# Two of GT's token tiles change places, and q's raw weights are loaded behind the first loads of Wv and Wo

## The chip, the cores and the metric

The kernel is one program on one core of a Trainium2 chip. The metric is the device time of one execution in microseconds, as the median of the runs. Names of engines are those of the profile: PE is TensorE's matmuls, PEld its weight loads, DVE is VectorE, ACT ScalarE, POOL GpSimd and SP SyncE, which in this kernel only issues DMAs.

## The reference

All tensors are float32; S = 2048 tokens, D = 640 channels, F = 1536, and 32 heads of 20 channels.

```
g = sigmoid((x * gate_w).sum(-1, keepdims=True))
q, k, v = heads of x @ wqkv
pq, pk = phi(q), phi(k)          # phi(t) = where(t > 0, t + 1, exp(t)) + 1e-6
kv = einsum("bhsd,bhse->bhde", pk, v);  z = sum of pk over the tokens
a = (pq @ kv / (pq . z + 1e-6), heads joined) @ wo
b = (sigmoid(x @ w_gate) * (x @ w_up)) @ w_down
out = g * a + (1 - g) * b
```

## The kernel before

The products run on PE in three passes each: an operand is split into a high part (a copy on ACT, line 420) and a low part (the difference, on DVE, line 424), and high*high, high*low and low*high are summed in PSUM (`mm3`, lines 407 to 409). Most of the large products are cut into blocks in Strassen's manner (seven block products), which needs sums of blocks on DVE ahead of the splits.

Instead of forming v, the kernel forms GT = x^T phi(k), of 640 x 640, from token tiles, and multiplies by Wv afterwards: kv = Wv^T GT for each group of heads. M = kv Wo then stands for the whole way from phi(q) to the output. The program goes like this:

1. phi(k) is formed for 16 token blocks of 128 rows. For each there is a token tile of 4 x 640 floats in each partition: the split x and the split phi(k). A pool `p1` holds six of these, with the tags tok0 to tok5, side by side in SBUF in this order; `token_tile()` hands them out in turn by a list of six tags.
2. GT is summed in batches. The last batch (c = 3) works on six token tiles: two of block 5, two of block 6, two of block 7. It goes over GT's seven pieces (five of 128 rows and two strips) for block 5 first, then over all seven for block 6, then over all seven for block 7. Each pass over the pieces is what lets go of a block's token tiles.
3. The pool `p1` is closed, and its memory is given to the pools of the next stage: `pw` and `pw2` (weights and intermediate tiles) and `mp` (Wv, Wo and kv). A tile there has to wait for the last reader of the token tile that lay in its place. In `mp` lie, from the bottom up, three buffers for Wv's groups (`wv_sb`), two for Wo's (`wo_sb`), then Wo's split parts (`woh`, `wol`), then kv's parts (`kvt`, `kvh`, `kvl`). `wst` in `pw2` holds raw weights: those of q first, then those of the gated unit.
4. The next stage starts with q for token groups 2 and 3 (`q_unit`, tile `wg` as weights, `dd` and `rot` as PSUM), and mixed into this stand six times `kv_part` (ten small matmuls with `wv_sb`, line 1627; then DVE masks the result into `kvt` and splits it) and `m_part` (Wo's split parts times kv). `wo_split` makes `woh` and `wol` from `wo_sb` on ACT and DVE.

What PE, ACT and DVE do is written out in a fixed order, which a small planner (`Order`) decides as the program is built, by estimated times for each engine. Each engine takes its instructions in that order, and a wait holds all that stands behind it. SP's queue is a list as well: the DMAs are issued in the order in which they stand, and one that waits for a tile to come free holds the ones behind it. In the built program an engine waits for a count in a semaphore; a DMA on SP also waits for the eighth DMA before it.

Around the change, SP's queue holds these loads: `xz` (x for the next chunk), `wg` and `w` (split and raw weights of q, the last ones that belong to GT's stage), then q's raw weights `wst`, then three loads of Wv (`load_mv`), two of Wo (`load_mo`), then `ws` and `wu` (q's other split weights) and a second `wst`. The line `sp.t = max(sp.t, freed)` sets only the planner's own estimate of when SP gets there.

Of the kernel before, what the change touches and what calls it, by code (L numbers as in the profile page):

```python
# [365 lines left out]
P_LAG, A_LAG, V_LAG = 0.2, 0.18, 0.14  # L366
# [8 lines left out]
def gated_mix_kernel(ctx: ExitStack, tc: tile.TileContext, xt, xn, wk, wv, wo, wst_q, wst_f, out_t):  # L375
# [6 lines left out]
    order = Order()  # L382
    rings = Rings()
    sp, gp = Ring(nc.sync, order, rings, 0, 0.38, 1.5), Ring(nc.gpsimd, order, rings, 1, 0.55, 2.2)
# [105 lines left out]
    tok_n = []  # L490

    def token_tile(dt=F32R):

        tag = f"tok{(0, 3, 1, 4, 2, 5)[len(tok_n) % 6]}"
        tok_n.append(0)
        return p1.tile([P, 4, D], dt, name="tok", tag=tag)

# [185 lines left out]
    for n in range(6):  # L683
        p1.tile([P, 4, D], F32, name="first", tag=f"tok{n}")
    st = [token_tile(F32).rearrange("p a b -> p (a b)") for _ in range(2)]
    k3h, k3l = (p1.tile([P, 2, HW], F32R, name=n, tag="kr", bufs=5) for n in ("k3h", "k3l"))
    wk_st = [st[k // 3][:, k % 3 * 2 * HW:(k % 3 + 1) * 2 * HW] for k in range(KC)]
# [66 lines left out]
    def queue_ls():  # L754

        p, w = FC // 2 - 1, 4 * P
        wd_dram[p] = dram.tile([P, 2, WF], F32, name=f"wd{p}")
        raw = qs.tile([P, 2, D], F32, name="qraw", tag="qraw")[:, :, :w]
        for j in range(2):
            sp.dma_start(raw[:, j], wst_f[2 * p + j, :, 2, :w])  # L760
        (a11, a21), (a12, a22) = [raw[:, j].rearrange("p (q h c) -> h p q c", q=2, h=2) for j in range(2)]

        def sums(part):
            if part == 0:
                add(a22, a21, a22)
                sub(a21, a11, a21)
            else:
                sub(a11, a22, a11)
                sub(a12, a12, a11)

        high = {}

        def form(j, q):
            if q == 0:
                high[j] = qs.tile([P, 2, 2 * P], F32R, name="qp", tag="qp", bufs=2)
            src = raw[:, j, 2 * q * P:2 * (q + 1) * P]
            split(high[j][:, q], src.bitcast(F32R), src)
            if q:
                cs = slice(2 * D + j * w, 2 * D + (j + 1) * w)
                order.then(lambda: [gp.dma_start(wd_dram[p][:, i, cs], t) for i, t in  # L780
                                    enumerate((f32(high[j]).rearrange("p q c -> p (q c)"), raw[:, j]))])
        for part in range(2):
            order.add(0, 2 * v_cost(2 * P), lambda part=part: sums(part), "qw", None, kept=True)
        for j in range(2):
            for q in range(2):
                order.add(a_cost(2 * P), v_cost(2 * P), lambda j=j, q=q: form(j, q), "qw", None, kept=True)
# [54 lines left out]
    def split_xn(n):  # L841
        i = tok(n // 2, n % 2)
        if i not in TOK:
            TOK[i] = token_tile()
        XN[i] = (TOK[i][:, 0], TOK[i][:, 1])
        split(*XN[i], xn_st.pop(n)[0])
        order.then(lambda: load_xn(n + 3))
# [118 lines left out]
    def k_split(i, after=""):  # L966
        r = KR.pop(i)
        if i not in TOK:
            TOK[i] = token_tile()
        PK[i] = (TOK[i][:, 2], TOK[i][:, 3])  # L970
        vh, vl = (t.rearrange(view2, j=2) for t in PK[i])
        act(vh, r, AF.Copy, after, bias=EPS)
        at = order.act + A_LAG

        def low():
            order.vec = max(order.vec, at)
            vec3(vl, r, EPS, f32(vh), OP.add, OP.subtract)
        order.then(low)
# [151 lines left out]
    for c in range(1, 4):  # L1130
# [102 lines left out]
        if c == 3:  # L1233
            for u in range(first, NU):
                g.part(u, 0, 2, ("cc", "dd", "rot", "cc")[u - first])
                order.fill()
            freed = order.pe + P_LAG
        for u in range(NU):
            g.part(u, 2 if u in g.ps else 0, 4, ("rot", "dd", "ch", "cc", "dd", "rot", "rot")[u])
            order.fill()  # L1240
# [2 lines left out]
            if c == 2 and u == NU - 1:  # L1243
                queue_ls()
    order.need(("xn", 7))
    order.need(("pk", 7))

    for u in (KC, KC + 1, 1):
# [36 lines left out]
    def load_form(n, i):  # L1285
        t = (wg_tile, wu_tile, ws_tile)[i]()
        w = t.shape[2]
        for c0, c1 in ((0, 2 * P), (7 * P, w), (5 * P, 7 * P), (2 * P, 5 * P)) if n == ("f", 0, 0) and i == 2 else ((0, w),):
            sp.dma_start(f32(t[:, :, c0:c1]), w_dram[n[::2] + (i,)][:, :, c0:c1])
        put(n, i, t)  # L1290
# [6 lines left out]
    def load_w():  # L1297
        t = pw2.tile([P, 2, D], F32, name="wst", tag="wst", bufs=2)
        if not w_loads:
            t = t.rearrange("p k c -> p (k c)").rearrange("p (k c) -> p k c", c=CW)  # L1300
            sp.dma_start(t, xt[len(c1_x), :, :, CW:])
            c1_x.append(t)
            other[-1].at = order.when(t)
            return
        n = w_loads.pop(0)
        sp.dma_start(t, wst_f[n[2], :, 0:2] if n[0] == "f" else wst_q[:, 0:2])
        WST[n] = t
        W_AT[n] = t
# [245 lines left out]
            for g in gs2:  # L1554
                order.add(0, v_cost(TG), lambda g=g, u=u: one(g, u), "den", lambda g=g, u=u: order.when(st[g, u]) + 1.5, chain=True)

    sp.t = max(sp.t, freed)
    load_w()
    mp_cm = tc.tile_pool(name="mp", bufs=1, reuse_waits="tile")
    mp = mp_cm.__enter__()  # L1560
    MV, MO, MO_AT, ZP = {}, {}, {}, []
# [1 line left out]
    def hg_slice(hg):  # L1563
        h0, h1 = HG[hg:hg + 2]
        return h0 * DH, (h1 - h0) * DH
# [8 lines left out]
    def load_mo(hg):  # L1574
        if hg < NHG:
            c0, w = hg_slice(hg)
            o = mp.tile([bdn, D], F32, name="wo_sb", tag="wo_sb", bufs=2)
            sp.dma_start(o[:w], wo[c0:c0 + w])
            MO[hg] = o
            MO_AT[hg] = o[:w]  # L1580
# [75 lines left out]
    load_mv(2)  # L1656
    load_mo(0)
    load_mo(1)
    sp.t = max(sp.t, order.pe + P_LAG)
    load_form(("q", 1, 2), 2)  # L1660
    load_form(("q", 1, 2), 1)
# [1401 lines left out]
```

## Time and profile before

| | |
|---|---|
| median of 3 runs | 730.3 us (730.19 to 730.45) |
| the profiled execution: its own time | 731.26 us |
| the profiled execution: its span, first to last instruction | 729.5 us |
| PE busy | 720.3 us, 99% of the span, 3395 matmuls |
| DVE / ACT / POOL busy | 583.0 us (80%) / 370.7 us (51%) / 117.2 us (16%) |
| mean granted clock of TensorE | 0.998 |
| data moved by DMA | 191.95 MB, 263 GB/s in the mean |

A row of the timeline is: start, duration, engine, line, operation, output <- inputs, shape, and in brackets the idle time of the engine before it and what ended it. The three rows of one product (lines 407, 408, 409) overlap in the record, since matmuls are pipelined; the distance from start to start is what a matmul costs. "issue" on SPq is the time in which the queue handles the DMA, not the transfer. DMA share is the mean busy share of the core's 16 DMA engines.

### The profile page before, as it was taken

To read this page: it belongs to the slowest core of one execution; us is meant where nothing else is said; L and a number is where in the kernel's file an instruction comes from. 1 tells how busy PE (TensorE), PEld (TensorE's weight loads), DVE (VectorE), ACT (ScalarE), POOL (GpSimd) and SP (SyncE) were. 2 spreads that over 40 slices of the span, in tenths; PEclk is the share of its full clock that TensorE was granted. 3 is DMA by queue.
4 is the path that set the end of the run, shared out by engine and by line. 5 is a ranking of instruction groups with operands and counts; after the bars stand their busy time and mean duration, and the time that the engine had idled before them with its cause. 6 is when DMAs were issued, how large, how long until landed. Compare 5 with 4: busy or idle time off the path is not lost.

```text
span 729.5 us, 9892 instructions
## 1 busy us (share of the span) xinstructions
PE 720.3 (99%) x3395; PEld 606.1 (83%) x3395; DVE 583.0 (80%) x1009; ACT 370.7 (51%) x685; POOL 117.2 (16%) x189
## 2 busy tenths in 40 slices
PE   9999999989999999999999999999999999999998
PEld 7999898768788888888888888888888888888886
DVE  6888878767768889898989987347696968799895
ACT  6784748148646763635354854355423242444451
POOL 0211113213320221311211134001010101002200
PEclk9999999999999999999999999999999999999999
DMA  7677688696967866757787979968989895959957
GB/s 249 167 217 191 179 200 249 181 318 233 342 228 273 313 230 243 274 207 271 272 294 284 299 269 354 411 236 276 356 251 302 270 396 175 409 216 333 213 105 238
DMA packets 78889, 191.95 MB, mean 263 GB/s; under 512 B 8394, under 2 KB 37018, under 8 KB 75126
## 3 DMA queue, kind: packets, MB, share of 16 engines
q1 hardware_dynamic: 57654, 117.72, 49.2%
q0 software_dynamic: 20896, 73.36, 30.0%
q8 instruction: 27, 0.44, 0.2%
q10 hardware_dynamic: 288, 0.23, 0.1%
q14 instruction: 24, 0.20, 0.1%
HBM read 113.46 MB, written 75.52 MB: 259 GB/s over the span
## 4 chain that ended last, share of the span: by engine, by line
PE 91%; issue 3%; DMA 2%; DVE 1%; POOL 1%; ACT 1%; SPq 0%; POOLq 0%; DVEq 0%; ACTq 0%
PE ch L408 10%; PE ch L407 10%; PE ch L409 10%; PE cc L407 8%; PE cc L409 8%; PE cc L408 8%; PE dd L407 6%; PE dd L408 6%; PE dd L409 6%; PE rot L407 5%; PE rot L409 5%; PE rot L408 5%; DMA wo_sb<-wo 1%; DMA p_dram<-qe 1%; PE dd L2788 1%
## 5 line engine op out<-in xcount | busy, mean ns | idle before, releaser
L420 ACT ACTIVATE c<-ch 128x512 f32<-128x512 f32 x54 | 32.2, 596 | 82.0 <-PE ch L409 81.7
L424 DVE TENSOR_TENSOR hf<-c,hf 128x512 fp32r<-128x512 f32 x80 | 54.4, 686 | 19.3 <-ACT hf L420 18.9
L420 ACT ACTIVATE hf<-c 128x512 fp32r<-128x512 f32 x80 | 48.9, 624 | 31.1 <-DVE c L424 31.0
L424 DVE TENSOR_TENSOR c<-cc,c 128x512 f32<-128x512 f32 x42 | 28.9, 688 | 26.4 <-PE cc L409 16.8
L407 PE MATMUL ch<-xth,ws 128*128 128x512 f32 x112 | 43.8, 391 | 0.1
L408 PE MATMUL ch<-xtl,ws 128*128 128x512 f32 x112 | 43.6, 390 | 0.0
L409 PE MATMUL ch<-xth,ws 128*128 128x512 f32 x112 | 43.6, 389 | 0.0
L424 DVE TENSOR_TENSOR c<-c,c 128x512 f32<-128x512 f32 x52 | 35.7, 686 | 3.3 <-ACT c L420 2.7
L424 DVE TENSOR_TENSOR tb<-rot,tb 128x512 f32<-128x512 f32 x56 | 36.1, 680 | 0.4 <-PE rot L409 0.4
L407 PE MATMUL dd<-xrh,wg 128*128 128x512 f32 x90 | 35.2, 391 | 0.0
L408 PE MATMUL dd<-xrl,wg 128*128 128x512 f32 x90 | 35.1, 389 | 0.0
L409 PE MATMUL dd<-xrh,wg 128*128 128x512 f32 x90 | 35.0, 389 | 0.0
L420 ACT ACTIVATE c<-dd 128x512 f32<-128x512 f32 x22 | 13.1, 598 | 41.1 <-PE dd L409 41.1
L407 PE MATMUL cc<-xbh,ws 128*128 128x512 f32 x84 | 32.8, 390 | 0.0
L408 PE MATMUL cc<-xbl,ws 128*128 128x512 f32 x84 | 32.7, 389 | 0.0
L409 PE MATMUL cc<-xbh,ws 128*128 128x512 f32 x84 | 32.7, 389 | 0.0
L424 DVE TENSOR_TENSOR tb<-dd,tb 128x512 f32<-128x512 f32 x36 | 24.7, 686 | 9.3 <-PE dd L409 9.3
L420 ACT ACTIVATE dd<-ch 128x512 f32<-128x512 f32 x22 | 12.8, 582 | 35.9 <-PE ch L409 35.9
L424 DVE TENSOR_TENSOR tb<-cc,tb 128x512 f32<-128x512 f32 x36 | 24.4, 683 | 1.9 <-PE cc L409 1.9
L424 DVE TENSOR_TENSOR wst<-wst 128x256 f32<-128x256 f32 (+1 forms) x65 | 24.6, 395 | 1.4
L407 PEld LDWEIGHTS ch<-xth,ws 128*128 128x128 f32 x112 | 21.0, 188 | 4.8 <-ACT c L420 0.7
L409 PEld LDWEIGHTS ch<-xth,ws 128*128 128x128 f32 x112 | 21.0, 188 | 4.7 <-DVE ws L424 0.3
(690 smaller groups left out, 2330.0 us busy)
## 6 DMA issues: line engine op xcount, KB each, us to landing
wf<-ws POOLq DMA_DIRECT2D x12, 1152.0 KB, 7.7
ws<-wf SPq DMA_DIRECT2D x11, 1152.0 KB, 8.1
wst<-wst_f SPq DMA_DIRECT2D x12, 640.0 KB, 5.1
wf<-wg POOLq DMA_DIRECT2D x12, 640.0 KB, 7.4
wd<-wd POOLq DMA_DIRECT2D x12, 640.0 KB, 7.5
wg<-wf SPq DMA_DIRECT2D x12, 640.0 KB, 6.6
wf<-wd SPq DMA_DIRECT2D x10, 640.0 KB, 10.3
xnst<-xn SPq DMA_DIRECT2D x16, 320.0 KB, 3.8
```

What stands on the lines that cost most here:

```text
L407: nc.tensor.matmul(out, l_hi, r_hi, start=first, stop=False, skip_group_check=True)
L408: nc.tensor.matmul(out, l_hi, r_lo, start=False, stop=False, skip_group_check=True)
L409: nc.tensor.matmul(out, l_lo, r_hi, start=False, stop=last, skip_group_check=True)
L420: nc.scalar.activation(out, src, fn, **kw)
L424: nc.vector.tensor_tensor(out, a, b, op=op)
L2788: nc.tensor.matmul(ps, l, r, start=new, stop=j == 1 and k == ks[-1], skip_group_check=True)
```

## The change

Three edits that belong together:

- In the list of tags, 1 and 2 change places. Block 6's first token tile moves from tok1 to tok2, and block 7's first one from tok2 to tok1 (each tag still follows itself after six tiles, so that what a token tile waits for is as before). In SBUF, the place of `wst` reaches over the end of tok2 and the start of tok3; tok3 holds block 5's second tile in both kernels. Wv's and Wo's buffers lie below tok0 and over tok0, which is block 5's first tile in both. Wo's split parts lie over tok1.
- `load_w()`, which loads q's raw weights into `wst`, goes behind the three loads of Wv and the two of Wo.
- The planner's estimate for SP is now set in two steps, one for the Wv and Wo loads (after block 5's pass) and one for q's raw weights (after block 6's pass).

```
-        tag = f"tok{(0, 3, 1, 4, 2, 5)[len(tok_n) % 6]}"
+        tag = f"tok{(0, 3, 2, 4, 1, 5)[len(tok_n) % 6]}"
...
-            freed = order.pe + P_LAG
+            freed = [order.pe + P_LAG]
...
     order.need(("xn", 7))
+    freed.append(order.pe + P_LAG)
     order.need(("pk", 7))
...
-    sp.t = max(sp.t, freed)
-    load_w()
+    sp.t = max(sp.t, freed[0])
     mp_cm = tc.tile_pool(name="mp", bufs=1, reuse_waits="tile")
...
     load_mv(2)
     load_mo(0)
     load_mo(1)
+    sp.t = max(sp.t, freed[1])
+    load_w()
     sp.t = max(sp.t, order.pe + P_LAG)
     load_form(("q", 1, 2), 2)
```

The order of the instructions on PE, DVE, ACT and POOL is the same in both kernels; the only rows that move are on SP. The piece of SP's queue around the change, at the end of GT's stage, with the semaphores each DMA waits for: PE and DVE are the engines' own counts, DMAHW0 to DMAHW7 the eight counts of SP's DMAs in turn; `w_1426` is the last raw weight tile of GT's stage.

```order
 L364 DMA w_1426<-wst_q 128x640 [waits DMAHW1_49,DVE_49]
-L364 DMA wst<-wst_q 128x1280 [waits DMAHW2_49,DVE_49,PE_49]
-L364 DMA wv_sb<-wv 128x600 [waits DMAHW3_49]
-L364 DMA wv_sb<-wv 128x600 [waits DMAHW4_49]
-L364 DMA wv_sb<-wv 128x500 [waits DMAHW5_49]
+L364 DMA wv_sb<-wv 128x600 [waits DMAHW2_49]
+L364 DMA wv_sb<-wv 128x600 [waits DMAHW3_49,PE_49]
+L364 DMA wv_sb<-wv 128x500 [waits DMAHW4_49]
+L364 DMA wo_sb<-wo 120x640 [waits DMAHW5_49]
 L364 DMA wo_sb<-wo 120x640 [waits DMAHW6_49]
-L364 DMA wo_sb<-wo 120x640 [waits DMAHW7_49]
+L364 DMA wst<-wst_q 128x1280 [waits DMAHW7_49,PE_49]
```

One DMA, `wst`, has moved behind five. Before, it stood in front and waited for PE and DVE; the counts in the program are those of block 7's tile in tok2: its last matmul in GT's row piece 3, fourth from the end of all of GT's matmuls. Now the first wait for PE stands at the second Wv load, and its count is that of block 5's first tile in the second strip, the last use of tok0. `wst` itself waits for the last use of tok2 by block 6, in the second strip too.

PE reads Wv's buffers right behind the first q unit (`dd_1623` is its PSUM tile), where the two first `kv_part` stand (`rot_1653` and `rot_1670`).

```order
 L409 MATMUL dd_1623<-xrh,wg 128x512
-L1627 MATMUL rot_1653<-gt,wv_sb 120x120 [waits DMAHW3_49,DVE_49]
+L1627 MATMUL rot_1653<-gt,wv_sb 120x120 [waits DMAHW2_49,DVE_49]
 L1627 MATMUL rot_1653<-gt,wv_sb 120x120
 L1627 MATMUL rot_1653<-gt,wv_sb 120x120 [waits DVE_49] x2
 L1627 MATMUL rot_1653<-gt,wv_sb 120x120
-L1627 MATMUL rot_1670<-gt,wv_sb 120x120 [waits DMAHW4_49,PE_49]
+L1627 MATMUL rot_1670<-gt,wv_sb 120x120 [waits DMAHW3_49,PE_49]
 L1627 MATMUL rot_1670<-gt,wv_sb 120x120 x4
 L407 MATMUL dd_1684<-xrh,wg 128x512 [waits Activation_49]
```

Nothing moves here: the two groups wait for the same loads as before, under the number of another semaphore.

More of the change, by code (lines that the diff above doesn't have):

```diff
@@ L492, in token_tile @@
     def token_tile(dt=F32R):
-        tag = f"tok{(0, 3, 1, 4, 2, 5)[len(tok_n) % 6]}"
+        tag = f"tok{(0, 3, 2, 4, 1, 5)[len(tok_n) % 6]}"
         tok_n.append(0)
@@ L1236, in gated_mix_kernel @@
                 order.fill()
-            freed = order.pe + P_LAG
+            freed = [order.pe + P_LAG]
         for u in range(NU):
@@ L1245, in gated_mix_kernel @@
     order.need(("xn", 7))
+    freed.append(order.pe + P_LAG)
     order.need(("pk", 7))
@@ L1555, in queue_dens @@
                 order.add(0, v_cost(TG), lambda g=g, u=u: one(g, u), "den", lambda g=g, u=u: order.when(st[g, u]) + 1.5, chain=True)
-    sp.t = max(sp.t, freed)
-    load_w()
+    sp.t = max(sp.t, freed[0])
     mp_cm = tc.tile_pool(name="mp", bufs=1, reuse_waits="tile")
@@ L1658, in gated_mix_kernel @@
     load_mo(1)
+    sp.t = max(sp.t, freed[1])
+    load_w()
     sp.t = max(sp.t, order.pe + P_LAG)
```

## The prediction

> **What bounds the kernel now.** I read the waits of PE first: all that ended an idle time of PE, in total, times, longest.
>
> ```profile
> PE rot L407 <- DVE kvt L424: 2.7, 1, 2.7
> PE rot L1627 <- DMA wv_sb<-wv: 1.7, 2, 1.4
> PE ch L407 <- ACT cx L420: 0.4, 1, 0.4
> ```
>
> PE is busy for nearly all of the span, and its two largest waits, 2.7 and 1.7 us, are for `kvt` and `wv_sb`: the place that the change touches. Next, the stretches around it: busy time of each engine, granted clock, share of the DMA engines, GB/s.
>
> ```profile
> 142.00:154.00 12.00, 7.57 (x43) 5.88 (x42) 4.09 (x10) 4.74 (x9) 0.00 (x0) 1.00 1.04 322
> 154.00:158.00 4.00, 4.00 (x12) 3.13 (x11) 3.93 (x9) 1.82 (x4) 0.57 (x1) 0.57 0.88 280
> 158.00:200.00 42.00, 41.53 (x217) 34.60 (x216) 33.40 (x66) 30.32 (x56) 13.13 (x24) 1.00 0.82 292
> ```
>
> From 142 to 154 PE works 7.57 of 12 us, with DVE and ACT idle as well and the DMA engines full: a stage that waits for transfers. Right behind it PE is busy but granted 0.57 of its clock; after that the clock is whole again. The timeline of PE there:
>
> ```profile
> 142.59 0.39 PE L409 MATMUL dd<-xrh,wg 128*128 128x512 f32 x1
> 144.42 1.28 PE L1627 MATMUL rot<-gt,wv_sb 128*120 128x120 f32 x10 [1.45 <-DMA wv_sb<-wv]
> 145.99 1.28 PE L1627 MATMUL rot<-gt,wv_sb 128*120 128x120 f32 x10 [0.28 <-DMA wv_sb<-wv]
> 147.03 0.47 PE L407 MATMUL dd<-xrh,wg 128*128 128x512 f32 x1
> ...
> 150.33 0.39 PE L409 MATMUL dd<-xah,wg 128*128 128x512 f32 x1
> 153.42 0.50 PE L407 MATMUL rot<-xbh,wg 128*128 128x512 f32 x1 [2.70 <-DVE kvt L424]
> ...
> 158.56 1.04 PE L1627 MATMUL cc<-gt,wv_sb 128*100 128x100 f32 x10
> ```
>
> The first wait is for Wv's loads themselves. For the second, I followed the engines behind `kvt`. DVE and ACT:
>
> ```profile
> 140.72 0.68 DVE L424 TENSOR_TENSOR gt<-cc,gt 128x512 f32<-128x512 f32 x1
> ...
> 142.71 0.69 DVE L424 TENSOR_TENSOR xtl<-xz,xth 128x512 fp32r<-128x512 f32 x1
> 151.15 0.83 DVE L424 TENSOR_TENSOR wol<-wo_sb,woh 120x640 fp32r<-120x640 f32 x1 [7.75 <-ACT woh L420]
> ...
> 153.09 0.28 DVE L424 TENSOR_TENSOR kvt<-rot,bd 120x120 f32<-120x120 f32 x1
> ```
>
> ```profile
> 142.58 0.58 ACT L420 ACTIVATE c<-ch 128x512 f32<-128x512 f32 x1
> 150.37 0.74 ACT L420 ACTIVATE woh<-wo_sb 120x640 fp32r<-120x640 f32 x1 [7.22 <-DMA wo_sb<-wo]
> ```
>
> ACT stands 7.22 us at `woh`, for Wo's load; DVE stands 7.75 us at `wol` behind it, and `kvt`, which needs neither, is queued after `wol`. PE's next unit needs the PSUM slot that `kvt` reads. So a late Wo load reaches PE through two in-order queues. In the chain that ended last it is the longest link:
>
> ```profile
> 141.44 8.91 DMA wo_sb<-wo
> ```
>
> Why the loads are late is in SP's queue:
>
> ```profile
> 122.92 0.38 SPq L364 DMA_DIRECT2D w<-wst_q  x1
> 138.93 0.33 SPq L364 DMA_DIRECT2D wst<-wst_q  x1
> 139.31 1.37 SPq L364 DMA_DIRECT2D wv_sb<-wv  x3
> 140.72 1.11 SPq L364 DMA_DIRECT2D wo_sb<-wo  x2
> 141.95 0.40 SPq L364 DMA_DIRECT2D ws<-wq  x1
> ```
>
> After `w` at 122.92 the queue stands for 15.6 us at `wst`, which waits for block 7's tile; the five loads wait only because they are behind it.
>
> **The change part by part.** *The five loads.* The second Wv load now waits for block 5's last matmul on tok0, `wst` for block 6's last on tok2. These are the first row and the second one here:
>
> ```profile
> 121.76 0.28 PE L409 MATMUL cc<-tok 128*128 128x256 f32 x1
> ...
> 130.36 0.28 PE L409 MATMUL cc<-tok 128*128 128x256 f32 x1
> ```
>
> The first ends at 122.04, before `w` is issued; so the five go out right behind `w`, from 123.3, in 1.37 + 1.11 us of issue and small gaps: by 126. Their 1450 KB (300, 300, 250 and twice 300, from the shapes) come behind what SP's queue still has in flight. The DMA engines' share there, per 10 us:
>
> ```profile
> 120.00:130.00 10.00, 10.00 (x51) 8.71 (x50) 9.05 (x12) 8.16 (x13) 1.23 (x2) 1.00 0.97 260
> 130.00:140.00 10.00, 10.00 (x53) 8.73 (x52) 7.73 (x13) 1.37 (x2) 2.62 (x4) 1.00 0.42 85
> ```
>
> Up to 130 they are full (0.97 at 260 GB/s), then 0.42. `w` has landed when ACT's split of it starts, at 130.66 (row below); 1450 KB at 260 GB/s take 5.7 us more: all five are there by about 136.4 (estimate from these rows). They are needed at 142.8. Nothing of that load time is on PE's path, before or after; the cover is 6.4 us.
>
> *q's raw weights.* `wst` can go at 130.64 instead of 138.93, 8.3 us earlier in spite of five DMAs in front. Its split on ACT comes behind both `woh`, so this costs nothing. `ws`, `wu` and the second `wst` still wait for GT's last matmul, but no longer for the issues of six DMAs ahead of them (138.93 to 141.95). A gain that PE doesn't see, since no wait of PE for `ws` is in the list above. No DMA is added, and POOL's queue isn't touched.
>
> *The tile swap.* It adds one wait: `woh` and `wol` now lie over block 7's tile, whose last matmul ends at 138.9 (`wst` was released by it, at 138.93). ACT gets to `woh` at 143.2, behind `c` (142.58 + 0.58). Cost nothing, with 4.3 us of cover.
>
> *The sum on PE,* from start to start. A matmul of the unit at 147.03 takes (150.33 - 147.03) / 14 = 0.236 us, a unit of 15 takes 3.53.
> - The first `kv_part` could start at 142.59 + 0.23 = 142.82; GT's last addition, which it needs too, ends at 141.40. It starts at 144.42: 1.60 us.
> - From the first to the second `kv_part` are 1.57 us, from the second, of the same size, to the next unit 1.04: 0.53 us.
> - The `rot` unit could start at 150.33 + 0.23 = 150.56; it starts at 153.42: 2.86 us.
> - That unit takes 158.56 - 153.42 = 5.14 us instead of 3.53: 1.61 us, the low clock.
>
> Together 6.60 us. Does `kvt` come in time? ACT starts `woh` at 143.2 instead of 150.37, DVE `wol` at 143.9 instead of 151.15: 7.2 us earlier. `kvt` follows at 153.09 - 7.2 = 145.9, and the unit that needs it starts at 142.82 + 1.04 + 1.04 + 3.53 = 148.4. 2.5 us of cover.
>
> The last term hangs on the low clock being the stall's own. The row: the clock is 0.57 only behind the longest wait of the kernel, and the 1.45 us wait left none. [...]
>
> *What is late next.* After 158 all three engines are where they were, PE 6.6 us earlier, DVE and ACT 7.2. The rest follows PE: the loads and stores there wait for tiles that PE, ACT or DVE let go. So the 6.6 us should reach the end of the span. The profiled span is 729.5, the median of the runs 730.3, 0.8 above it: 729.5 - 6.6 = 722.9, and **730.3 - 6.6 = 723.7 us**.
>
> **The rivals.**
>
> *A, the low clock stays* although the waits go: 5.0 us are left, **725.3 us**. For it: the clock falls behind a wait of only 2.70 us, and the small matmuls of `kv_part` stay. Against: the later ones, the one at 158.56 among them, lie in stretches at 1.00.
>
> *B, a new wait of DVE takes the old one's place.* DVE's train from `wol` has no gap, and PE needs its end:
>
> ```profile
> 164.80 0.68 DVE L424 TENSOR_TENSOR c<-dd,c 128x512 f32<-128x512 f32 x1
> ...
> 165.60 0.35 PE L407 MATMUL dd<-woh,kvh 120*120 120x320 f32 x1
> ```
>
> PE takes that PSUM slot 0.12 us after DVE is done with it. From `wol` to the end of this `c` are 165.48 - 151.15 = 14.33 us; from 143.9 on, the end is 158.2, against 159.0 for PE's need (165.60 - 6.6). Each us over 0.8 that DVE loses to ACT in between is lost to PE; with twice that, 1.6, the gain is 5.8: **724.5 us**.
>
> *C, the gain is given back.* The chain that ended last has a later link:
>
> ```profile
> 185.52 5.12 DMA p_dram<-qe
> ```
>
> ACT waits for that store, and PE's third wait, 0.4 us, ends behind it. If this chain kept its place in time, the wait would grow to 7.0 us: **730.3 us**. Against: POOL issues that store behind DVE's `qe`, which comes from PE's products, so that it moves along.
>
> *D, the loads don't go early,* the place of Wv's buffers being held by something that I overlook. They would go at 138.93 instead of 139.31, and without 640 KB in front (2.5 us at 260 GB/s). That still takes 0.4 + 2.5 of the waits and the 1.6 of the clock: **725.8 us**.
>
> *E, slower: `w` lands late.* The five loads share the engines with `w`, whose split stands on ACT and DVE ahead of GT's last additions:
>
> ```profile
> 130.66 0.74 ACT L420 ACTIVATE wg<-w 128x640 fp32r<-128x640 f32 x1 [2.42 <-DMA w<-wst_q]
> 135.69 0.78 DVE L424 TENSOR_TENSOR wg<-w,wg 128x640 fp32r<-128x640 f32 x1
> ```
>
> DVE takes it at 135.69, so 135.69 - 0.74 - 130.66 = 4.3 us are free; then 1.42 more, to GT's last addition (141.40 against 142.82). Beyond 136.4 each us is lost, and the gain is gone when `w` lands after 143.0, 20.1 us after its issue instead of 7.7. At three times 7.7, it would be 146.1: 3.1 us slower, **733.4 us**. If all 1450 KB came before `w`'s last byte, it would land at 136.4: still free. [...]
>
> **How the numbers follow.** The forecast has 0.78, A 0.06, B 0.08, C 0.03, D 0.02, E 0.03. Range: below, the forecast with PE's third wait gone too and 0.3 for the sizes of the terms, 723.0; above, A with as much again, 725.6; C, D and E (0.08) are left out, and the rest of the 2 in 10 is in my terms. What a measurement of this kernel can tell from no change is about 0.2%, 1.5 us; the forecast, A, B and D lie beyond: faster 0.94, same (C) 0.03, slower (E) 0.03.
>
> **What would show it.** Right: SP issues Wv and Wo from 123 to 126 and `wst` at about 130.7; ACT's `woh` starts near 143 with no wait for a DMA; PE's waits for `wv_sb` and `kvt` are gone; the clock is 1.00 from 142 to 158; the third `kv_part` starts near 152.0 instead of 158.56, and from there all rows stand 6.6 us earlier to the end. Wrong: a clock under 1 there (A), a PE wait for DVE's `c` near 159 (B), a larger wait near 193 (C), Wv's issue still near 139 (D), ACT's split of `w` after 136 (E).

## The result, and the profile after

| | before | after |
|---|---|---|
| median of the runs, us | 730.38 (730.19 to 730.73, 4 runs) | 724.12 (723.36 to 724.72, 4 runs) |
| profiled execution: time, span, us | 731.26, 729.5 | 723.36, 721.6 |

The ratio is 0.9913, 95% interval 0.9896 to 0.993: 6.3 us faster, by the interval 5.1 to 7.6. 723.7 us had been forecast. The profiled execution before lies above all the runs of its kernel (0.9 us above their median), the one after is the fastest of its own (0.8 below), so their spans differ by more, 7.9 us.

The waits of PE in the profile after, in total, times, longest:

```profile
PE rot L502 <- PEq L3056: 0.8, 1, 0.8
PE ch L407 <- ACT cx L420: 0.3, 1, 0.3
PE ch L1064 <- DVE k1h L867: 0.2, 1, 0.2
```

The waits for `kvt` (2.7) and `wv_sb` (1.7) are gone; what leads the list now is 0.8 us of PE's own sequencer ahead of its first matmul. That wait stood in the kernel before too, as did the 0.2 us for `k1h`; the prediction's list, said to be all of them, leaves both out, so that its "third wait" of 0.4 us is the fourth. The stretches around the change, in the columns of before (busy time of PE, PEld, DVE, ACT, POOL, then clock, DMA share, GB/s):

```profile
142.00:154.00 12.00, 12.00 (x72) 10.38 (x71) 10.86 (x22) 7.66 (x14) 3.88 (x7) 1.00 1.01 339
154.00:158.00 4.00, 4.00 (x21) 3.47 (x20) 3.80 (x11) 2.16 (x4) 0.54 (x1) 1.00 0.69 258
158.00:200.00 42.00, 41.72 (x212) 34.99 (x211) 31.90 (x60) 29.92 (x55) 12.69 (x23) 1.00 0.82 291
```

From 142 to 154 PE is busy for 12.00 of 12 us instead of 7.57, and the 0.57 in the clock column has become 1.00. The same stretch on PE's timeline (a row of 20 is both `kv_part`s, one right behind the other):

```profile
142.80 2.26 PE L1627 MATMUL rot<-gt,wv_sb 128*120 128x120 f32 x20
144.82 0.48 PE L407 MATMUL dd<-xrh,wg 128*128 128x512 f32 x1
145.13 0.40 PE L408 MATMUL dd<-xrl,wg 128*128 128x512 f32 x1
...
148.31 0.39 PE L407 MATMUL rot<-xbh,wg 128*128 128x512 f32 x1
...
151.72 1.04 PE L1627 MATMUL cc<-gt,wv_sb 128*100 128x100 f32 x10
```

Read start against start, each row gives a term. The first `kv_part` stands at 142.80 instead of 144.42 (1.62 earlier), the unit behind the second at 144.82 instead of 147.03 (2.21, so 0.59 more), the `rot` unit at 148.31 instead of 153.42 (5.11, so 2.90 more), the third `kv_part` at 151.72 instead of 158.56 (6.84, so 1.73 more). SP's queue:

```profile
122.99 0.38 SPq L364 DMA_DIRECT2D w<-wst_q  x1
123.43 1.39 SPq L364 DMA_DIRECT2D wv_sb<-wv  x3
124.87 1.06 SPq L364 DMA_DIRECT2D wo_sb<-wo  x2
130.65 0.36 SPq L364 DMA_DIRECT2D wst<-wst_q  x1
```

The five loads go out 16 us earlier than before, and `wst` 8.3 us earlier although it stands behind them. ACT and DVE, which had stood at `woh` and `wol` for 7.22 and 7.75 us:

```profile
131.09 0.74 ACT L420 ACTIVATE wg<-w 128x640 fp32r<-128x640 f32 x1 [3.07 <-DMA w<-wst_q]
...
143.02 0.73 ACT L420 ACTIVATE woh<-wo_sb 120x640 fp32r<-120x640 f32 x1
```

```profile
135.66 0.78 DVE L424 TENSOR_TENSOR wg<-w,wg 128x640 fp32r<-128x640 f32 x1
...
143.78 0.83 DVE L424 TENSOR_TENSOR wol<-wo_sb,woh 120x640 fp32r<-120x640 f32 x1 [0.41 <-ACT woh L420]
...
145.72 0.28 DVE L424 TENSOR_TENSOR kvt<-rot,bd 120x120 f32<-120x120 f32 x1
...
157.95 0.69 DVE L424 TENSOR_TENSOR c<-dd,c 128x512 f32<-128x512 f32 x1
```

`woh` starts at 143.02 without a wait for Wo, `kvt` at 145.72; it ends at 146.00, 2.3 us ahead of its reader's need at 148.31. The last row matters below: this `c` ends at 158.64.

### The profile page after: what moved, and what is told of

It reads as the page before. It is cut to its first block, busy times and chain, and to the rows that moved or that the text cites. A ratio compares the mean times of both kernels' runs of the same rounds, so it can differ in the third digit from the quotient of the medians.

```text
span 721.6 us, 9893 instructions
## 1 busy us (share of the span) xinstructions
PE 717.0 (99%) x3395; PEld 605.3 (84%) x3395; DVE 583.1 (81%) x1009; ACT 370.3 (51%) x685; POOL 117.0 (16%) x189
## 4 chain that ended last, share of the span: by engine, by line
PE 93%; DVE 2%; ACT 2%; DMA 1%; issue 1%; DVEq 0%; ACTq 0%
PE ch L407 10%; PE ch L408 10%; PE ch L409 10%; PE cc L407 8%; PE cc L408 8%; PE cc L409 8%; PE dd L408 7%; PE dd L407 7%; PE dd L409 7%; PE rot L407 5%; PE rot L409 5%; PE rot L408 5%; DMA wo_sb<-wo 1%; PE dd L2790 1%; DVE wst L424 1%
## 5 line engine op out<-in xcount | busy, mean ns | idle before, releaser
L409 PEld LDWEIGHTS ch<-xth,ws 128*128 128x128 f32 x112 | 21.0, 188 | 4.7 <-DVE ws L424 0.3
L408 PEld LDWEIGHTS ch<-xtl,ws 128*128 128x128 f32 x112 | 21.0, 188 | 4.3
```

Source lines behind the costliest of these rows:

```text
L408: nc.tensor.matmul(out, l_hi, r_lo, start=False, stop=False, skip_group_check=True)
L409: nc.tensor.matmul(out, l_lo, r_hi, start=False, stop=last, skip_group_check=True)
```

## The experiments

The theory was the one of the prediction: the five loads are late only because they stand in SP's queue behind `wst`, and Wo's lateness reaches PE through ACT's and DVE's queues. The rivals were that the tile swap does the work, or only one of the two weights counts; that the low clock has a cause of its own; and that DVE's later work (`c`, rival B) is next. Four kernels take the change apart, two hold `kvt` back without any DMA. The first four were timed beside the kernel before on one chip (before: 730.86 there, 9 runs), the last three on another (730.83, 13 runs). Diffs are against the changed kernel.

**The order alone** (the tags as before):

```
-        tag = f"tok{(0, 3, 2, 4, 1, 5)[len(tok_n) % 6]}"
+        tag = f"tok{(0, 3, 1, 4, 2, 5)[len(tok_n) % 6]}"
```

> The tags as before, only the load of q's raw weights behind the five. The place in the queue is enough: Wv and Wo go at 123 to 126 as in the changed kernel; q's raw weights still wait for block 7 (138.9), but with no load in front of them they land about 4 us later, before ACT's split of them at 145.3. PE has no wait for Wv or kvt, the clock is whole, the time is that of the changed kernel, 724.1 (730.4 - 6.3) within 0.5. The rival, that the swap is needed too (q's raw weights, late among ws, wu and the second wst, hold ACT and DVE behind their split): 725 to 727, with an ACT wait for wst of 1 us or more and a PE wait after 152.

Measured: 723.69 us (723.21 to 723.94), ratio 0.9905 (0.9891 to 0.9918). SP's queue in it:

```profile
123.14 1.83 SPq L364 DMA_DIRECT2D wv_sb<-wv  x3
125.01 1.77 SPq L364 DMA_DIRECT2D wo_sb<-wo  x2
138.92 0.36 SPq L364 DMA_DIRECT2D wst<-wst_q  x1
```

`wst` goes as late as before, and the time is that of the whole change: the order alone gives all of it, and `wst`'s earlier issue is worth nothing, as forecast (ACT's split of it starts at 145.33 without a wait).

**The swap alone** (the tags of the changed kernel, `load_w()` back in front of `load_mv` and `load_mo`):

```
-            freed = [order.pe + P_LAG]
+            freed = order.pe + P_LAG
...
-    freed.append(order.pe + P_LAG)
...
-    sp.t = max(sp.t, freed[0])
+    sp.t = max(sp.t, freed)
+    load_w()
...
     load_mo(1)
-    sp.t = max(sp.t, freed[1])
-    load_w()
```

> Only the tags swapped, q's raw weights still in front. They can go at 130.6 instead of 138.9, and the five behind them at once, 131.0 to 133.7. 640 + 1450 KB at the 284 GB/s that the changed kernel moved from 130 to 140 take 7.5 us: all landed by about 138.5, before 142.8. If what counts is only that the loads no longer stand behind block 7, the time is 724.1 again, within 0.5, and each half of the change does all of it alone. The rival, that the place in front matters: Wo lands after 143.0, ACT waits for it, 725 to 727.

Measured: 723.89 us (723.49 to 724.9), ratio 0.991 (0.9897 to 0.9924). SP's queue:

```profile
131.22 0.33 SPq L364 DMA_DIRECT2D wst<-wst_q  x1
131.60 1.37 SPq L364 DMA_DIRECT2D wv_sb<-wv  x3
133.01 0.93 SPq L364 DMA_DIRECT2D wo_sb<-wo  x2
```

Here the five loads still stand behind `wst`, but the head of the queue is let go 7.7 us earlier (131.22 against 138.93), and that is enough: no wait for `wv_sb`, `woh` or `kvt` is left. So the halves of the change don't add up; each does the whole, one by passing the head of the queue, the other by freeing it.

**Wv alone in front** (old tags; the queue is Wv, `wst`, Wo) and **Wo alone in front** (Wo, `wst`, Wv). The diff of the first; the second moves `load_mv` instead:

```
-        tag = f"tok{(0, 3, 2, 4, 1, 5)[len(tok_n) % 6]}"
+        tag = f"tok{(0, 3, 1, 4, 2, 5)[len(tok_n) % 6]}"
...
-    load_mo(0)
-    load_mo(1)
     sp.t = max(sp.t, freed[1])
     load_w()
+    load_mo(0)
+    load_mo(1)
```

> The tags as before; the queue is Wv, q's raw weights (which wait until 138.9), Wo. Takes only the first wait of PE away. Wo's loads go at 139.3 as before, but without Wv's 850 KB in front: they land about 3 us earlier than at 150.35, near 147.3, so kvt comes near 150.0 and PE waits 1.7 us instead of 2.86. If the low clock belongs to a wait of a certain length, 1.7 is near the 1.45 that left it whole: 724.1 + 1.7 = 725.8. If any such wait brings it: 727.4. Nothing gained from Wv alone (the two waits are one): 730.

Measured: 726.61 us (725.68 to 727.25), ratio 0.9948 (0.9934 to 0.9961). DVE and PE in it:

```profile
146.50 0.83 DVE L424 TENSOR_TENSOR wol<-wo_sb,woh 120x640 fp32r<-120x640 f32 x1 [2.98 <-ACT woh L420]
...
160.15 0.68 DVE L424 TENSOR_TENSOR c<-dd,c 128x512 f32<-128x512 f32 x1
```

```profile
148.77 0.50 PE L407 MATMUL rot<-xbh,wg 128*128 128x512 f32 x1 [0.15 <-DVE kvt L424]
...
160.89 0.41 PE L407 MATMUL dd<-woh,kvh 120*120 120x320 f32 x1 [1.23 <-DVE c L424]
```

ACT, where `woh` waits for Wo's load:

```profile
145.73 0.74 ACT L420 ACTIVATE woh<-wo_sb 120x640 fp32r<-120x640 f32 x1 [2.46 <-DMA wo_sb<-wo]
```

The expectation missed. Wo was there sooner than it had said (ACT starts `woh` at 145.73, where it had said 147.3 and the kernel before had 150.37), so hardly a wait for `kvt` is left, 0.15 us; but DVE, which started its train at 146.50, ends `c` at 160.83, and PE stands 1.23 us for it. That is rival B's wait, at its place.

> The tags as before; the queue is Wo, q's raw weights (wait until 138.9), Wv. Takes only the second wait away: ACT's woh starts near 143 to 145 with no wait for a DMA. PE waits for Wv as before (landing near 144.4 and 146), together 2.1 us, then nothing, with a whole clock: 724.1 + 2.1 = 726.2. If the low clock came from the Wv wait or from the small matmuls and not from the second wait, it stays: 727.9.

Measured: 725.1 us (724.66 to 726.32), ratio 0.9929 (0.9917 to 0.9942). PE's timeline:

```profile
144.22 2.33 PE L1627 MATMUL rot<-gt,wv_sb 128*120 128x120 f32 x20 [1.07 <-DMA wv_sb<-wv]
...
153.24 1.04 PE L1627 MATMUL cc<-gt,wv_sb 128*100 128x100 f32 x10
```

One wait for Wv is left, 1.07 us, smaller than expected and none for the second `kv_part`; there is no wait for `kvt`, and the clock is 1.00 from 142 on. The first `kv_part` starts 0.20 us sooner than before (144.22 against 144.42), though Wv was issued 0.20 us later; that Wo's 600 KB no longer share the DMA engines with it fits this, but wasn't tried by itself. The third `kv_part` is 1.52 us behind the changed kernel's, and the time 1.4 us above that of the order alone. Of the two weights, Wo is the one that matters more by the medians (725.1 with Wo early, 726.61 with Wv early); the intervals of the two overlap a little (up to 0.9942, from 0.9934).

**The changed kernel again**, beside the two stalls:

> The changed kernel once more, on the chip of the next two: 724.1 within 0.7; PE without a wait from 142 to 158, clock 1.00 there.

Measured: 723.84 us (723.21 to 724.37), ratio 0.9907 (0.9891 to 0.9923). PE has no wait from 142 to 158, and the clock is 1.00 there.

**Two stalls at `kvt`**, of 12 and of 17 repeats: DVE repeats the first masking into `kvt`, from the same operands to the same result, so that `kvt` is late while every load is early.

```
+        for _ in range(12 if hg == 0 else 0):
+            nc.vector.tensor_tensor(kvt[:w, :w], ps[:w, :w], bd.rearrange("p b c -> p (b c)")[:w, :w], op=OP.mult)
```

> The changed kernel, with the first masking of kvt made 13 times instead of once (the same result each time): 12 more of about 0.30 us on DVE in front of PE's release, no DMA touched. kvt ends near 149.6 instead of 146.0, PE waits 0.30 x 12 - 2.3 = 1.3 us. Clock whole, since the wait is under 1.45: 724.1 + 1.3 = 725.4. If DVE's later work becomes the bound as well, more.

Measured: 726.75 us (726.53 to 727.97), ratio 0.995 (0.9934 to 0.9966). PE's waits, DVE's late `c`, and PE's rows: the `rot` unit behind the wait for `kvt`, the third `kv_part` behind that unit, and the row that waits for `c`:

```profile
PE rot L407 <- DVE kvt L1632: 1.4, 1, 1.4
PE dd L407 <- DVE c L424: 1.2, 1, 1.2
```

```profile
161.25 0.69 DVE L424 TENSOR_TENSOR c<-dd,c 128x512 f32<-128x512 f32 x1
```

```profile
149.86 0.50 PE L407 MATMUL rot<-xbh,wg 128*128 128x512 f32 x1 [1.38 <-DVE kvt L1632]
...
153.42 1.04 PE L1627 MATMUL cc<-gt,wv_sb 128*100 128x100 f32 x10
...
161.99 0.41 PE L407 MATMUL dd<-woh,kvh 120*120 120x320 f32 x1 [1.24 <-DVE c L424]
```

A wait of 1.38 us at `kvt`, the clock 1.00 from 142 on, and again a wait of 1.2 for `c`. The 725.4 had left that second wait out; the expectation's proviso on DVE's later work is what came.

> The same with 17 more: PE waits 0.30 x 17 - 2.3 = 2.8 us, as long as the wait that the change removed, but for DVE and with all loads early. If the low clock follows from the length of the wait, it comes back (0.57 for about 3.5 us): 724.1 + 2.8 + 1.7 = 728.6. [...]

Measured: 728.59 us (727.96 to 729.66, 9 runs), ratio 0.9973 (0.9964 to 0.9983). PE's timeline, the stretch behind the wait (columns as above), and DVE's `c`:

```profile
151.28 0.59 PE L407 MATMUL rot<-xbh,wg 128*128 128x512 f32 x1 [2.96 <-DVE kvt L1632]
151.68 0.63 PE L408 MATMUL rot<-xbl,wg 128*128 128x512 f32 x1
152.10 0.63 PE L409 MATMUL rot<-xbh,wg 128*128 128x512 f32 x1
...
156.41 1.04 PE L1627 MATMUL cc<-gt,wv_sb 128*100 128x100 f32 x10
...
163.43 0.39 PE L407 MATMUL dd<-woh,kvh 120*120 120x320 f32 x1
```

```profile
152.00:154.00 2.00, 2.00 (x6) 1.51 (x6) 1.94 (x5) 0.00 (x0) 0.00 (x0) 0.50 0.03 8
```

```profile
162.67 0.68 DVE L424 TENSOR_TENSOR c<-dd,c 128x512 f32<-128x512 f32 x1
```

The wait is back without a late load, and the low clock with it: 0.50 from 152 to 154, matmuls 0.43 us apart instead of 0.23, and the unit takes 156.41 - 151.28 = 5.13 us, as it took 5.14 before the change. The time is the one that the expectation gave, 728.6, but that is luck in part: it had added 2.8 us of wait and 1.7 of low clock along PE, and DVE's `c` is late by 163.35 - 158.64 = 4.71 us in any case. PE has no wait for `c` here; by these rows it would have come earlier with a whole clock, and waited for `c`. One of the nine executions has a mean clock of 1.000, so the clock didn't fall in it, and it took 728.35 us, in the middle of the others.

## Why the prediction was right

**The loads.** Issue at 123.43 to 125.93, as forecast (from 123.3, by 126). Rival E didn't come: ACT's split of `w` starts at 131.09 instead of 130.66, and DVE's where it was (135.66). One line of the prediction is wrong as it stands: that nothing of the five loads' time is on PE's path "before or after". Before, it was on the path, which is what the change removes. D is excluded by SP's rows. The premise that the loads wait only for the head of the queue is shown twice: by the order alone, which passes it, and by the swap alone, which frees it.

**The sum.** At the third `kv_part` 6.84 us were gained where 6.60 had been worked out: 1.62 for 1.60, 0.59 for 0.53, 2.90 for 2.86, 1.73 for 1.61. Half of what is missing is in the last: I had taken a unit at 3.53 us, from a unit behind a `kv_part`, whose first matmul takes longer to be followed (144.82 to 145.13, 0.31 against 0.23); a unit in full run takes 151.72 - 148.31 = 3.41. So the 1.73 aren't the low clock alone either: a unit behind a wait takes 153.42 - 149.86 = 3.56 at a whole clock (12 repeats), which leaves 5.14 - 3.56 = 1.58 for it. From there the gain goes on to the end, so C falls (PE's third wait went from 0.4 to 0.3); the profiled execution adds 1.1 us further on, in small steps that I have not traced one by one. The whole change gave 6.3 and 7.0 us by the medians on the chips it was timed on, its halves 7.2 and 7.0: around 6.8, each known to about 1 us.

**The low clock.** Rival A falls: the clock is 1.00 from 142 on in the changed kernel and in all its parts, with the small matmuls of `kv_part` in place. The long stall brings it back with no DMA involved, so it belongs to the stall, as I had taken it. It doesn't come in every execution, though, and for this the mean clock of each is on record. The 3.4 us at half rate of the profiled execution before make its mean 0.998. Of the 22 executions of the kernel before that were timed beside the experiments, 11 have 0.998 or less and 11 have 0.999 or 1.000; of the 9 with 17 repeats, 8 have 0.998 or less; of the 31 of all the other kernels, none. In the traces the clock fell to 0.50 behind the waits of 2.70 and 2.96 us, and stayed at 1.00 behind those of 1.07, 1.38 and 1.45. What a wait between 1.45 and 2.70 does, and what decides in a single execution, no run here tells.

**What the sum had wrong: the slack of B.** I gave DVE's `c` 0.8 us of slack: 14.33 us from `wol` to its end, against PE's need at 159.0. It was 0.10: `c` ends at 158.64 (14.86 from `wol`, since with a faster PE the train now has a gap: DVE stands 0.4 us for ACT at one `qe`), and PE starts at the slot at 158.74:

```profile
153.03 0.69 DVE L428 SCALAR_TENSOR_TENSOR qe<-qe,qr 128x512 f32<-128x512 f32 x1 [0.43 <-ACT qr L420]
```

```profile
158.74 0.36 PE L407 MATMUL dd<-woh,kvh 120*120 120x320 f32 x1
```

It cost nothing in the changed kernel, but it missed by little, and it is what both misses of the experiments have in common. Set beside the changed kernel, at this place:

| kernel | clock of the `rot` unit | end of `c`, later by | PE's `dd<-woh,kvh`, later by |
|---|---|---|---|
| Wv alone | 1.00 | 160.83, 2.19 | 160.89, 2.15 |
| 12 repeats | 1.00 | 161.94, 3.30 | 161.99, 3.25 |
| 17 repeats | 0.50 for 3.4 us | 163.35, 4.71 | 163.43, 4.69 |
| before | 0.50 for 3.4 us | 165.48, 6.84 | 165.60, 6.86 |

PE is late here by what DVE is late, whether it lost that time in a wait for `kvt`, at a low clock, or in a wait for `c`. And DVE doesn't depend on the clock here: from the start of the first `kvh`, its step behind `kvt`, to the end of `c` it takes 12.08 and 12.10 us in the two kernels with a whole clock (148.75 to 160.83, 149.84 to 161.94), and 12.09 and 12.08 in the two with a low one (151.26 to 163.35, 153.40 to 165.48). So the 6.6 us can be read along DVE as well: `wol` started 151.15 - 143.78 = 7.37 us late, 0.5 of that was made up, 6.84 were left. The terms of my sum are right as places where PE's time went, but the last one wasn't a gain of its own: had only the low clock gone, PE would have come to `dd` about 1.6 us earlier, at 164.0, and stood there until 165.5 for `c`. That reading is worked out from the rows and the table, and the executions bear it out: the 11 of the kernel before whose clock fell took 730.8 us in the mean, the 11 whose clock didn't 730.9. None of these 22 left a trace, so that their waits aren't seen. That the sum along PE came within 0.3 us of the 6.84 is therefore luck in part: at its low clock PE was late by just as much as DVE was.

## What to carry to other kernels

When a queue issues in order, look at its head first: either move the needed loads past it or let the head go earlier, and expect one of the two to do the whole, as each did here (723.69 and 723.89 us, against 724.12 with both). Follow a late load through every in-order engine up to the one that sets the time, and then further to that engine's next need of the late one: where two chains end within 0.1 us of each other, as PE's and DVE's do here, the terms along one of them add up to the gain only if the other chain comes earlier as well. A low clock behind a long wait belongs to the price of the wait (about 1.6 us along PE here, behind 2.70 and 2.96 us), but it may be covered by that second chain, as it was before the change, and in single executions it may not come at all (in 11 of 22 of the kernel before and 1 of 9 with 17 repeats, by the mean clock): look at the mean clock of all the executions, not of the profiled one alone.

## What the runs showed of the hardware

- PE idle for 2.70 and 2.96 us brought a low clock in the profiled executions, and idle times of 1.45 us and less did not. Before, in steps of 0.2 us, the clock is 0.91 from 154.2 to 154.4, 0.50 from there to 157.6 and 0.56 from 157.6 to 157.8: it falls 0.9 us after the first matmul behind the wait (153.42) and stays at 0.50 for 3.4 us. With 17 repeats it is 0.88 from 150 to 152, 0.50 from 152 to 154 and 0.76 from 154 to 156; at 0.50 throughout, that is a fall 0.2 us after the first matmul (151.28) and again 3.4 us. The unit with 17 repeats loses 5.13 - 3.56 = 1.57 us by it.
- It does not come in each execution: by the mean clock (0.998 or less), it came in 11 of 22 of the kernel before (2.70 us of wait in its trace) and in 8 of 9 with 17 repeats (2.96 us in its trace).
- What 1450 KB issued right behind `w` cost it can't be told. ACT's split of `w`, which waits for it, starts 7.74 us after its issue before (130.66 - 122.92) and 8.10 us in the changed kernel (131.09 - 122.99), with the DMA engines full in both (share 0.97 and 0.98 from 120 to 130, the second below); but it starts 7.34 us after it (122.52) with 17 repeats, which has the same loads behind `w`. In the two kernels DVE did not have to wait for that split: it takes its part at 135.69 and 135.66.

```profile
120.00:130.00 10.00, 10.00 (x51) 8.73 (x50) 9.05 (x12) 8.02 (x13) 1.31 (x2) 1.00 0.98 265
```
